# The block of w_q that lies on few partitions: 32 partitions and 4 steps instead of 16 and 8

## The chip, the cores and the metric

The kernel runs on one core of a Trainium2 chip. The metric is the device time of one execution in microseconds (us). A measured change of 2% in either direction counts as faster or slower.

## What is computed

One decode step for two sequences (B = 2) of width D = 448: a layer norm, grouped-query attention over a cache of 4096 keys (16 query heads of 256, 8 key/value heads), a bilinear feed-forward block whose SiLU gates the attention's result, and a residual.

```python
xn = layernorm(x)                                   # x: (2, 1, 448)
q = (xn @ wq).reshape(2, 1, 16, 256)                # wq: (448, 4096)
p = softmax(q . k_cache * 256 ** -0.5)              # k_cache, v_cache: (2, 8, 4096, 256)
s = (p . v_cache).reshape(2, 1, 4096) @ wo          # wo: (4096, 448)
g = silu(((xn @ w_gate) * (xn @ w_up)) @ w_down)    # F = 1792
out = x + s * g
```

All data is float32, some 158.5 MB of it, and almost all of that is the two caches.

## The kernel before

Each of the 16 pairs (key/value head, sequence) is a step of the main loop. Step i needs the tile of its values and the tile of the next step's keys. Both come in one load of 8 MB, `vk[i]`, of 128 partitions by 64 KB, into a `ring` of two buffers. The weights come through one buffer, `slot`, one after the other: w_q for the first half of the heads (`wq0`), w_gate and w_up (`wgu`), w_down (`wd`), w_q for the second half (`wq1`), and w_o (`wo`). All these loads are issued by SyncE (SP) at line 73 in one fixed order, which is the list `todo` (lines 83 to 91): wq0, first keys, vk0, wgu, vk1, vk2, wd, vk3, vk4, wq1, vk5, vk6, vk7, vk8, wo, vk9 to vk13, and then the last keys and values in pieces. A load is issued when the buffer that it goes to is free, that is when the matmuls that read that buffer's former content are done. A load that has to wait keeps those behind it on SP waiting too.

The instructions of every engine stand in the order in which the code records them (a manual schedule). In step i of the loop (line 312) TensorE runs the matmuls of `values(i)` (line 269), those of `scores(i + 1)` (line 238) and the small ones of the softmax. Then the next `ring` load may go, since both halves of its buffer have been read. After step 4 comes `query(1)`, the projection of the second half of the heads, which reads `wq1` out of `slot`.

`query` calls `rows` (line 163). D = 448 is cut into 3 blocks of 128 rows (k = 0, 1, 2) and one of 64, and the 2048 columns of one half into NT = 4 blocks of 512, one for each group of 32 columns of the PE array, so that four matmuls of 32 output columns can be in the array beside each other. For the second half one of these blocks, k = 2 and c = 0 (rows 256 to 383), isn't loaded with the others. It isn't in `wq1`, which has 13 blocks instead of 14, and lies in DRAM in an array of its own, `wqx`, folded onto SIDE = 16 partitions and EXTRA = 8 steps. It is loaded behind `wq1`'s columns in the same buffer (line 77) and multiplied in 8 matmuls of 16 rows each (line 174), all in column group 0, with `xeT`, the transposed rows of xn that belong to them. `xeT` is written once at the start, by 8 transposes of TensorE (line 136) and a copy of VectorE (line 137).

In DRAM, `wqx` has groups of rows with a row of padding behind each group, so that the load's source has the groups as its outer dimension: 4 groups of 4 rows of 16 KB each.

Of the kernel before, what the change touches and what calls it, by code (L numbers as in the profile page):

```python
# [26 lines left out]
LATE = 24  # L27
THIRD = [24, 25, 26, 28, 29, 30, 31, 27]
PART = 28 * FC
EXTRA = 8  # L30
SIDE = 16
EPS = 1e-5


# [5 lines left out]
def gated_decode_block(ctx: ExitStack, tc: tile.TileContext, x, first, vk, last0, last1, wq0, wq1, wqx, wo, wgu, wd, out):  # L40
    nc = tc.nc
# [7 lines left out]
    def bank(name="t", bufs=1):  # L49
        return psum.tile([128, 512], F32, name=name, bufs=bufs)  # L50
# [8 lines left out]
    loaded = {}  # L59
    todo = []  # L60

    def issue(n=1):
        for names, src, cuts in todo[:n]:
            weight = names[0].startswith("w")
            if weight:
                t = slot.tile([128, PART], F32, name="slot", align_bytes=512)
            else:
                t = ring.tile([128, 2 * ROW], F32, name="ring", align_bytes=512)
            width = ROW if not weight else PART // len(names)
            for i, name in enumerate(names):  # L70
                loaded[name] = t[:, i * width:(i + 1) * width]
            for lo, hi in zip(cuts, cuts[1:]):
                nc.sync.dma_start(t[:, lo:hi], src[:, lo:hi])  # L73
            if names == ["wq1"]:
                at = src.shape[1]
                loaded["wqx"] = t[:, at:at + EXTRA * 512]
                nc.sync.dma_start(loaded["wqx"][:SIDE], wqx[:, :4])
        del todo[:n]

    def plan(names, src, cuts=None):  # L80
# [9 lines left out]
    plan(f"k{LAST + 1} v{LAST}", last0, [0, ROW, 2 * ROW])  # L90
    plan(f"v{LAST + 1} wo2", last1, [0, 4096, 7168, *(ROW + i * D for i in (0, 3, 5, 7, 8))])
    issue(3)


# [36 lines left out]
    oT1 = const.tile([128, 3, 2, REP, W], F32)  # L131
    xeT = oT1[:SIDE].rearrange("p g d r m -> p (g d r) m")[:, :EXTRA]
    pt = bank()
    for j in range(EXTRA):
        at = 256 + j * SIDE
        nc.tensor.transpose(pt[:SIDE, B * j:B * (j + 1)], xn[:, at:at + SIDE], ident[:B, :B])
    nc.vector.tensor_copy(xeT.rearrange("p k (b j) -> p k b j", b=B),
                          pt[:SIDE, :EXTRA * B].rearrange("p (k b) -> p k b", b=B)[:, :, :, None].to_broadcast([SIDE, EXTRA, B, DUP]))

# [23 lines left out]
    def rows(ps, w, n, extra=None):  # L163
# [6 lines left out]
        for k in range(3):  # L170
            for c in range(NT):
                if extra is not None and (k, c) == (2, 0):
                    for j in range(EXTRA):
                        nc.tensor.matmul(ps[:W, :n], xeT[:, j, :], extra[:SIDE, j * n:(j + 1) * n], start=False, stop=False)  # L174
                    continue
# [132 lines left out]
    oT2 = const.tile([128, 1, 2, REP, W], F32)  # L308
    ss = scores(0)
    issue(2)  # L310
    p = over(softmax(*ss))
    for i in range(LAST):
        g, b = divmod(i, B)
        o = bank("o", 1)
        values(i, p[0], o)
        ss = scores(i + 1)

        issue(1 + (i + 1 in weights))
        nc.scalar.activation(ob[:, b * 4 + g if g < 4 else b * 3 + g - 4], o, AF.Copy, scale=p[1])  # L319
        if i == LAST - 1:  # L320
            cb = combine(ob, 6)
        p = softmax(*ss)
        if i < LAST - 1:
            p = over(p)
        if i == 7:
            cb = combine(ob, 8)
            for n in range(B):
                turn(oT0, cb[:, n * 256:(n + 1) * 256], 0, n, 4)
            ob = work.tile([128, 8, 512], F32, name="ob", bufs=1)
        if i in weights:  # L330
            if i == 0:
                ffn_in()
            if i == 2:
                ffn_out()
            if i == 4:
                query(1)
            if i == 8:
                project(oT0, 0, 0, EARLY)
# [78 lines left out]
```

## Time and profile before

| | us |
|---|---|
| median of 3 runs | 377.04 (376.45 to 396.36) |
| the profiled execution's own time | 377.45 |
| its span, first to last instruction | 375.7 |
| TensorE busy | 218.1 (58% of the span) |
| VectorE busy | 63.4 (17%) |
| ScalarE busy | 36.3 (10%) |

The span is what the views of the profile divide up; 1.75 us of the execution's own time lie outside it. A float32 matmul shows as two matmul instructions, so the 8 matmuls of line 174 are counted as 16. A load is named in the views by the buffer that it writes and the array that it reads: `ring<-vk`, `slot<-wq`, `slot<-wqx`.

### The profile page before, as it was taken

The page shows a single profiled execution, that of the slowest core. Times are in us where ns is not written, and L with a number is a line of the kernel's source. Part 1 is how long each engine was busy: PE and PEld are TensorE (multiplying, and loading weights), DVE is VectorE, ACT ScalarE, POOL GpSimd, SP SyncE. Part 2 cuts the span into 40 slices and gives each one's busy share as a digit, 9 for nine tenths or more (in the row PEclk, how much of TensorE's full clock was granted, in tenths as well). Part 3 has the DMA queues.
Part 4 walks back from the last instruction along what each step waited for, and adds up shares of the span by engine and source line. Part 5 has one row for each costly group of instructions (what it writes and reads, how often), then busy time and mean ns, then how long its engine had stood idle before and what let it go on. Part 6 is the DMA issues. An engine that isn't in the chain of part 4 may idle for free.

```text
span 375.7 us, 3266 instructions
## 1 busy us (share of the span) xinstructions
PE 218.1 (58%) x1470; PEld 64.2 (17%) x1470; DVE 63.4 (17%) x113; ACT 36.3 (10%) x56; POOL 1.2 (0%) x7
## 2 busy tenths in 40 slices
PE   1650649083861919699783766622827181919785
PEld 1110112021210202121121212200212021202232
DVE  4012030103030030300213030300121112030330
ACT  1001010001012020100111010100010101010120
POOL 1000000000000000000000000000000000000000
PEclk9986697667786776655967788965858685768899
DMA  8999999998999999999999999999999999999994
GB/s 342 440 461 391 441 447 447 447 441 386 430 434 447 440 405 484 426 405 440 434 433 426 420 433 405 455 447 433 440 420 434 447 412 426 448 412 429 419 417 163
DMA packets 4246, 158.74 MB, mean 423 GB/s; under 512 B 503, under 2 KB 633, under 8 KB 1145
## 3 DMA queue, kind: packets, MB, share of 16 engines
q1 hardware_dynamic: 4228, 158.54, 98.1%
q8 instruction: 11, 0.18, 0.2%
q14 instruction: 3, 0.02, 0.0%
q10 hardware_dynamic: 4, 0.00, 0.0%
HBM read 158.54 MB, written 0.01 MB: 422 GB/s over the span
## 4 chain that ended last, share of the span: by engine, by line
DMA 71%; PE 25%; SPq 1%; DVE 1%; issue 0%; ACT 0%; ACTq 0%
DMA ring<-vk 66%; PE o L269 12%; PE s L238 7%; DMA ring<-last 6%; PE t L174 4%; PE t L176 1%; SPq L73 1%; PE t L179 0%; DVE m L239 0%; ACT p L253 0%; PE acc L302 0%; DVE mx L246 0%; PE sm L261 0%; DVE h L366 0%; PE sm L244 0%
## 5 line engine op out<-in xcount | busy, mean ns | idle before, releaser
L269 PE MATMUL o<-ring,pT 128*32 128x512 f32 x480 | 83.0, 854 | 80.1 <-DMA ring<-vk 79.3
L238 PE MATMUL s<-ring,qT 128*32 128x512 f32 x512 | 61.0, 618 | 4.8 <-DMA ring<-first 3.3
L239 DVE TENSOR_REDUCE m<-s 128x1 f32<-128x1024 f32 x16 | 19.6, 1225 | 211.6 <-PE s L238 211.6
L269 PEld LDWEIGHTS o<-ring,pT 128*32 128x32 f32 x480 | 21.0, 150 | 133.5 <-issue 132.7
L319 ACT ACTIVATE ob<-o,su 128x512 f32<-128x512 f32 x14 | 9.6, 688 | 194.9 <-PE o L269 194.9
L253 ACT ACTIVATE p<-s,m 128x1024 f32<-128x1024 f32 x16 | 17.8, 1114 | 94.5 <-DVE m L250 94.5
L238 PEld LDWEIGHTS s<-ring,qT 128*32 128x32 f32 x512 | 17.8, 114 | 45.6 <-issue 44.0
L255 DVE STREAM_TRANSPOSE pT<-p 128x1024 f32<-128x1024 f32 x16 | 19.9, 1245 | 22.5 <-ACT p L253 22.5
L261 PE MATMUL sm<-su,add_head 128*128 128x1 f32 x32 | 7.8, 312 | 22.9 <-ACT p L253 22.9
L244 PE MATMUL sm<-ident,m 128*1 128x128 f32 x16 | 4.3, 270 | 18.9 <-DVE m L239 18.8
L174 PE MATMUL t<-slot,oT 16*32 16x512 f32 x16 | 13.9, 1056 | 0.0
L176 PE MATMUL t<-slot,xnT 128*32 128x512 f32 x46 | 10.9, 1059 | 4.0 <-DMA slot<-wq 4.0
L246 DVE TENSOR_REDUCE mx<-sm 1x128 f32<-1x512 f32 x16 | 10.9, 679 | 6.3 <-PE sm L244 6.3
L249 PE MATMUL sm<-one,mx 1*128 1x1 f32 x16 | 3.6, 223 | 12.3 <-DVE mx L246 12.3
L261 PEld LDWEIGHTS sm<-su,add_head 128*128 128x128 f32 x32 | 6.4, 249 | 25.1 <-ACT p L253 24.1
L176 PE MATMUL s<-slot,xnT 128*32 128x448 f32 x48 | 7.2, 747 | 2.7 <-DMA slot<-wgu 2.7
L244 PEld LDWEIGHTS sm<-ident,m 128*1 128x1 f32 x16 | 1.3, 79 | 33.0 <-DVE m L239 32.3
L188 DVE STREAM_TRANSPOSE qT<-t 128x256 f32<-128x256 f32 x4 | 1.6, 428 | 31.0 <-PE t L179 31.0
L296 PE MATMUL wide<-slot,oT 128*32 128x448 f32 x48 | 6.6, 701 | 0.0
L278 PE MATMUL cb<-ob,add_blocks 128*32 128x64 f32 (+2 forms) x64 | 5.9, 496 | 0.8 <-ACT ob L358 0.8
L220 PE MATMUL t<-slot,hT 128*32 128x448 f32 x28 | 4.9, 810 | 0.0
L249 PEld LDWEIGHTS sm<-one,mx 1*128 1x128 f32 x16 | 2.2, 139 | 15.4 <-DVE mx L246 15.4
(68 smaller groups left out, 54.5 us busy)
## 6 DMA issues: line engine op xcount, KB each, us to landing
ring<-last SPq DMA_DIRECT2D x2, 4096.0 KB, 24.2
slot<-wgu SPq DMA_DIRECT2D x1, 6272.0 KB, 38.5
slot<-wo SPq DMA_DIRECT2D x1, 5376.0 KB
ring<-first SPq DMA_DIRECT2D x1, 4096.0 KB, 20.3
slot<-wq SPq DMA_DIRECT2D x1, 3584.0 KB, 11.0
slot<-wq SPq DMA_DIRECT2D x1, 3328.0 KB, 35.6
slot<-wd SPq DMA_DIRECT2D x1, 3136.0 KB, 36.9
ring<-last SPq DMA_DIRECT2D x1, 2048.0 KB
```

The costliest lines, as they stand in the source:

```text
L174: nc.tensor.matmul(ps[:W, :n], xeT[:, j, :], extra[:SIDE, j * n:(j + 1) * n], start=False, stop=False)
L176: nc.tensor.matmul(ps[W * c:W * (c + 1), :n], xnT[:, k, :], block(NT * k + c), start=k == 0, stop=False)
L238: nc.tensor.matmul(s[W * c:W * (c + 1), h, :], q[:, d], k[:, h, d, c, :], start=d == 0, stop=d == 1)
L239: nc.vector.tensor_reduce(m[:, 0:1], s, axis=AX.XY, op=OP.max)
L246: nc.vector.tensor_reduce(mx, sm[:1, None, :128].rearrange("p o (c j) -> p o j c", c=NT).to_broadcast([1, NT, W, NT]), axis=AX.X, op=OP.max)
L253: nc.scalar.activation(p, s, AF.Exp, bias=m[:, 1:2], scale=1.0 / 16, accum_out=su[:, 0:1])
L255: nc.vector.transpose(pT.rearrange("p h n -> p (h n)"), p.rearrange("p h n -> p (h n)"))
L261: nc.tensor.matmul(sm[:, 130:131], add_head.rearrange("p a r j -> p (a r j)"), su[:, 0:1], start=True, stop=True)
L269: nc.tensor.matmul(o[W * t:W * (t + 1), :], pT[:, h, at:at + 2 * W:2], loaded[f"v{i}"][:, e * 512:(e + 1) * 512], start=e < NT, stop=e >= ...
L278: nc.tensor.matmul(cb[W * c:W * (c + 1), :n * 64], add_blocks[:, e].rearrange("p r j -> p (r j)"), src[:, :n, e, :, c, :], start=e == 0, s ...
L296: nc.tensor.matmul(wide[W * t:W * (t + 1), :D], heads(oT, i, first), loaded["wo"][:, i * D:(i + 1) * D], start=i < NT, stop=i >= LATE - NT)
L319: nc.scalar.activation(ob[:, b * 4 + g if g < 4 else b * 3 + g - 4], o, AF.Copy, scale=p[1])
```

## The change

SIDE goes from 16 to 32 and EXTRA from 8 to 4, and the number of groups, which was SIDE // 4 = 4, gets a name of its own, GROUPS = 4. The block keeps its 128 rows by 512 columns, 256 KB. It is now 4 groups of 8 rows of 8 KB each, with one row of padding behind each group, on partitions 0 to 31. Four matmuls of 32 rows take the place of 8 of 16, and 4 transposes that of 8.

```diff
-EXTRA = 8
-SIDE = 16
+EXTRA = 4
+SIDE = 32
+GROUPS = 4
@@ issue
-                nc.sync.dma_start(loaded["wqx"][:SIDE], wqx[:, :4])
+                nc.sync.dma_start(loaded["wqx"][:SIDE], wqx[:, :SIDE // GROUPS])
@@ kernel
-    wqx = np.zeros((SIDE // 4, 5, EXTRA * 512), np.float32)
-    wqx[:, :4] = wq1[:, 8 * 512:9 * 512].reshape(EXTRA, SIDE // 4, 4, 512).transpose(1, 2, 0, 3).reshape(SIDE // 4, 4, EXTRA * 512)
+    n = SIDE // GROUPS
+    wqx = np.zeros((GROUPS, n + 1, EXTRA * 512), np.float32)
+    wqx[:, :n] = wq1[:, 8 * 512:9 * 512].reshape(EXTRA, GROUPS, n, 512).transpose(1, 2, 0, 3).reshape(GROUPS, n, EXTRA * 512)
```

The order of the instructions on every engine and the semaphores that each load waits for stay as they were.

## The prediction

> **What bounds the kernel now.** I read the page's slices and its table of DMA queues first, to see whether the transfers ever rest.
>
> ```profile
> DMA  8999999998999999999999999999999999999994
> q1 hardware_dynamic: 4228, 158.54, 98.1%
> q8 instruction: 11, 0.18, 0.2%
> DMA 71%; PE 25%; SPq 1%; DVE 1%; issue 0%; ACT 0%; ACTq 0%
> ```
>
> They don't: the 16 DMA engines are busy in every slice up to the last. Queue q1, which holds the loads, takes 98.1% of 16 engines' span. That is 0.981 x 375.7 x 16 = 5897 us of engine time for 158.54 MB, so one engine moves 26.9 KB per us and all sixteen 430 KB. The end comes when the engine with the most to do has done it. The chain of waits says 25% TensorE, but that is not time in which the transfers stood still. To see where TensorE's work reaches them I read the chain in order of time around the changed block.
>
> ```profile
> 156.17 3.57 PE t L176 x16
> 159.74 13.79 PE t L174 x16
> 173.53 1.86 PE t L176 x6
> 175.38 1.86 PE t L179 x8
> 177.25 3.87 PE o L269 x32
> 181.12 3.49 PE s L238 x32
> 184.61 0.02 issue
> 184.62 24.59 DMA ring<-vk
> ```
>
> Columns: start, length, what. Line 174, the block on few partitions, takes 13.79 us of TensorE, and the values and scores behind it (L269, L238) release a ring buffer only at 184.61. The load that goes there is vk7 in the order of the list: it is issued at 184.62 and has landed 24.59 us later. A vk load is 8.39 MB, 19.5 us at 430 KB per us, so 5.1 us are left for what stood before it and for the start. How long a start takes on idle engines is seen at the kernel's first load.
>
> ```profile
> 0.74 0.39 SPq L73
> slot<-wq SPq DMA_DIRECT2D x1, 3584.0 KB, 11.0
> ```
>
> The first load of w_q, 3.67 MB or 8.5 us of flow, landed 11.0 us after its issue, so 2.5 us go to the start and to the spread of the engines. Of vk7's 5.1 us that leaves 2.6 us of older work on the engine that finished last. The transfers were nearly out of work when it was issued. The windows of 5 us around it show it in the last column (GB/s):
>
> ```profile
> 164.00:169.00 5.00, 5.00 (x7) 0.97 (x6) 0.00 (x0) 0.00 (x0) 0.00 (x0) 0.50 0.97 419
> 179.00:184.00 5.00, 5.00 (x52) 1.32 (x44) 0.00 (x0) 0.69 (x1) 0.00 (x0) 1.00 0.99 423
> 184.00:189.00 5.00, 1.32 (x12) 0.50 (x4) 2.37 (x4) 1.21 (x2) 0.00 (x0) 0.91 0.97 367
> 189.00:194.00 5.00, 4.26 (x22) 1.37 (x26) 0.99 (x2) 0.00 (x0) 0.00 (x0) 0.50 0.97 419
> ```
>
> From 184 to 189 the flow is 367 against 419 to 423 on both sides: 54 x 5 = 270 KB fewer than at 421, or 0.6 us of all engines. It is a dip in a flow that is elsewhere steady, and the only place where TensorE's work in this kernel costs transfer time.
>
> **The change, part by part.** First TensorE.
>
> ```profile
> L174 PE MATMUL t<-slot,oT x16: 1056/1056/1057, 159.7 to 172.5; 16*32 16x512 f32 x16
> L176 PE MATMUL t<-slot,xnT x22: 1057/1057/1062, 156.1 to 174.3; 128*32 128x512 f32 x22
> L179 PE MATMUL t<-slot,xnT x8: 1057/1058/1059, 175.3 to 176.2; 64*32 64x512 f32 x8
> ```
>
> An instruction on 16, 64 or 128 rows takes the same (1056, 1058, 1057 ns), so one on 32 rows does too. The 16 instructions of line 174 follow each other in one column group, 13.79 / 16 = 0.86 us apart; 8 fewer take 6.9 us away. The values would then start at 177.25 - 6.9 = 170.3 if their load has landed.
>
> ```profile
> 113.95 0.33 SPq L73 DMA_DIRECT2D slot<-wq  x1
> 114.33 0.82 SPq L77 DMA_DIRECT2D slot<-wqx  x1
> 131.61 68.28 SPq L73 DMA_DIRECT2D ring<-vk  x4
> ring<-vk SPq DMA_DIRECT2D x2, 38.6
> slot<-wqx SPq DMA_DIRECT2D x1, 256.0 KB
> ```
>
> vk5 and vk6, the two of the fourth row, take 38.6 us in the median. vk5, issued at 131.61, lands near 170.2, just in time. The buffer comes free near 177.7, vk7 is issued 6.9 us earlier, and stands behind work that lasts some 9 us instead of 2.6. So the dip goes. Its worth lies between nothing (if it is only the grain of 64 KB rows in windows of 5 us) and the 2.5 us of a whole start. I take the measured 0.6 us as a mean over the engines, and 0.3 us for those that carried wqx, since their queue was the fuller one. Behind that the next thing late is the transfers themselves.
>
> The rest of what TensorE, VectorE and SP lose or gain is covered. The 4 transposes and the smaller copy lie at the start, where TensorE then waits 4.01 us for the first weights:
>
> ```profile
> 6.33 0.34 PE L136 MATMUL t<-ident,pT 2*16 2x2 f32 x8 [0.38 <-DVE xnT L127]
> 11.92 1.08 PE L176 MATMUL t<-slot,xnT 128*32 128x512 f32 x4 [4.01 <-DMA slot<-wq]
> ```
>
> They are worth at most 0.34 us, inside that wait; if the cover were gone they would be a gain of 0.2 us. The issue of wqx took SP 0.82 us from 114.33; with 32 rows instead of 16 it could take twice that, or less than now. SP's next issue comes at 131.61, so up to 16 us of cover stand behind it.
>
> Now the load itself, where the profile of before has no row for the new form. Its 256 KB stay 256 KB. Over four engines that is 65.5 KB each, 65.5 / 26.9 = 2.44 us; over sixteen it would be 0.61 us, over two 4.9 and over one 9.7 us. The 2.6 us that vk7's slowest engine still had in front of it are nearest to four, and exclude two and one. So today four engines run 2.44 us behind the others from the wqx load on. With 4 groups as the outer dimension again, I take four engines again, and as many bytes on each. What differs is where they write: 8 neighbouring partitions each instead of 4, and partitions 16 to 31 are new. While they do, the other twelve engines go on with vk5, each into its own partitions. If what limits the flow is the engine, an engine may write anywhere at 26.9 KB per us, and the price is 0. If what limits it is the receiving side, where two engines meet on the same partitions they have half of it each. Then an engine whose whole 65.5 KB are shared needs 4.88 us, 2.44 us more, and the engine that it meets loses 1.2 us. Those are the ends, 0 and +2.44 us on some of the four; every window shows a full flow with every engine in its own partitions, and so no row is near either end. I take the upper end, for two of the four engines: the rows of groups 2 and 3 go to partitions that no wqx row went to before, where other engines are writing vk5.
>
> The Trainium skill speaks against the change here: its page "SBUF — State Buffer", section "Door 1: The DMA port swizzle", says that four neighbouring partitions (with the four 32 above) lie behind one of 16 ports of about 27.2 GB/s each, and measures 27.6 GB/s for a load to partitions 0 to 3 and 104 GB/s for one to 0 to 15. By it the old load meets only the ports of its own engines, and the new one those of four others: the sum is then the upper end, and without it the lower one. No run here shows it yet.
>
> What of 2.44 us reaches the end is read from the last microseconds of transfer.
>
> ```profile
> 350.27 21.14 DMA ring<-last
> 371.40 0.04 issue
> 368.00:369.00 1.00, 0.73 (x6) 0.00 (x0) 0.00 (x0) 0.23 (x1) 0.00 (x0) 1.00 0.91 355
> 369.00:370.00 1.00, 0.49 (x28) 0.49 (x32) 0.00 (x0) 0.46 (x1) 0.00 (x0) 1.00 0.74 294
> 370.00:371.00 1.00, 1.00 (x40) 0.65 (x28) 0.25 (x1) 0.00 (x0) 0.00 (x0) 1.00 0.34 133
> 371.00:371.50 0.50, 0.13 (x8) 0.05 (x8) 0.00 (x0) 0.00 (x0) 0.00 (x0) 1.00 0.10 36
> ```
>
> From 368 on 355 + 294 + 133 + 18 = 800 KB flow, 1.9 us at 430. The mean engine thus ends near 369.9 and the last at 371.4: 1.5 us of slack for an engine in the middle, none for the last. The four carriers are among the late ones, since they had 2.44 us more to do; against that the 11 instruction fetches of q8 (0.2% of 5897 us, some 1 us each) fall on single engines too. An engine in the middle would push the end by 2.44 - 1.5 = 0.9 us, the last one by 2.44. I take the middle, 1.7 us, less the 0.3 us that the carriers gain at 184: +1.4 us. The work behind the last landing, from 371.4 to 375.7, is unchanged.
>
> Sum for the profiled execution: 377.45 + 1.4 = 378.85 us. That execution is 0.41 us above the median of the runs, 377.04, so I forecast 378.4 for the median.
>
> **Rivals.** First, faster: the receiving side isn't the limit and four engines write at full speed. For it speaks that no row of this trace shows two engines held up at one place; against it that none could, since every load so far gives each engine partitions of its own. Then only the dip at 184 goes: 377.04 - 0.6 = 376.4, with 376.0 to 376.8 for a gain of 0.3 to 1.0.
>
> Second, slower by more: the load falls on fewer engines than four. It decides as soon as one engine holds all of it: 9.7 us instead of 2.44, +7.3 us, less 0.9 of mean slack and gain is 6.4, so 383.4. For it speaks only that rows and groups are no longer equal in number (8 and 4); against it that the outer dimension is 4 as before. The Trainium skill, "DMA: Bandwidth & Descriptors", section "Why a DMA increments its semaphore by 16 and not by 1", gives a load the largest number of engines up to 16 that divides both outer dimensions, here 4 and 32, so 4 as with 4 and 16; the landing of vk7 agrees for the old one.
>
> Third, nothing shows: no sharing, and the dip at 184 stays because it comes with each late issue or is only grain: 377.0.
>
> **How the numbers follow.** The forecast with sharing has 0.64, the faster rival 0.28, no effect 0.05, fewer engines 0.03. The forecast's own range is 0.9 - 0.3 to 2.44 on the median, 377.6 to 379.5. To hold 8 in 10 the range takes in the faster rival down to 376.0 and ends at 379.5; what is left out is the fewer engines and the outer ends of the others. A measurement of this kernel can tell about 2%, 7.5 us, from no change. None of the main cases reaches that on either side: within 2% has 0.97. Faster by that would need the transfers to gain 7 us where the dip holds at most 2.5: 0.01. Slower by that needs the load on one engine and no slack at all: 0.02.
>
> **What would show it.** Line 174's matmuls, 8 instructions in some 6.9 us instead of 13.79. vk7 issued near 178 if vk5 lands at 170.2, near 180 if it lands 2.4 us later as sharing would have it. The window of 184 to 189 back at some 420 GB/s. The tail of the flow behind 370: with sharing longer and thinner by one to two us, the last landing near 372.8; without it the last landing near 370.8. The forecast is wrong if the tail ends earlier than now, and the whole reasoning is if the flow shows a stop elsewhere.

## The result

The changed kernel takes 378.83 us (median of 6 runs, 378.72 to 379.10) against 376.98 us for the kernel before, measured beside it: a ratio of 1.0048 with a 95% interval of 1.0033 to 1.0064. That is 1.8 us slower, clear of the noise and well inside 2%. The forecast was 378.4. One of the six runs of the kernel before took 396.36 us, a slow run that the ratio leaves out.

The profiled execution took 379.07 us, with a span of 377.3. Its flow of transfers first, in the windows around the load of wqx and around 184 us (columns: window, length, busy time and instructions of PE, PEld, DVE, ACT and POOL, clock, DMA share, GB/s). The kernel after:

```profile
147.00:153.00 6.00, 4.27 (x41) 1.11 (x33) 1.57 (x2) 0.69 (x1) 0.00 (x0) 1.00 1.12 348
184.00:189.00 5.00, 0.60 (x3) 0.43 (x3) 1.71 (x4) 1.20 (x2) 0.00 (x0) 0.79 0.97 419
```

The kernel before, in the first of these windows:

```profile
147.00:153.00 6.00, 4.66 (x44) 1.16 (x35) 1.22 (x1) 0.69 (x1) 0.00 (x0) 0.99 1.15 496
```

While wqx is loaded the flow is 348 GB/s instead of 496, 148 x 6 = 890 KB less in these 6 us, or 2.1 us of all engines at 430. (The view counts a transfer's bytes in one place, so that a window of a few us can be off by some 15%.) At 184, where the kernel before had 367, it is now 419: that dip is gone. The transfer records of the trace say the same more finely. They have the start, the length and the bytes of every row of a load, but don't name the engine. With the bytes spread evenly over each row's time, the flow in the first window is 316 GB/s instead of 432, or 1.6 us of all engines. From 147 to 154 the rows took 30.1 us of engine time more than rows of their size take undisturbed (2.42 us for a vk row of 64 KB), 1.88 us per engine, against 0.003 before; from 184 to 190 it was 0.003, against 0.63 before.

TensorE's side, from the chain of waits and the timeline of the kernel after:

```profile
131.18 41.77 DMA ring<-vk
172.95 0.14 issue
173.09 5.40 PE o L270 x32
178.49 3.47 PE s L239 x32
181.96 0.02 issue
181.98 29.57 DMA ring<-vk
```

```profile
155.47 2.97 PE L177 MATMUL t<-slot,xnT 128*32 128x512 f32 x16
158.36 7.03 PE L175 MATMUL t<-slot,oT 32*32 32x512 f32 x8
165.32 1.93 PE L177 MATMUL t<-slot,xnT 128*32 128x512 f32 x6
167.18 1.93 PE L180 MATMUL t<-slot,xnT 64*32 64x512 f32 x8
173.09 5.40 PE L270 MATMUL o<-ring,pT 128*32 128x512 f32 x32 [3.97 <-DMA ring<-vk]
```

The block on few partitions takes 7.0 us instead of 13.8, and the projection is done at 169.1. But vk5, issued at 131.18, lands only at 172.95, so that TensorE waits 4.0 us for it. The buffer comes free at 181.96, 2.65 us earlier than before, and the load that is issued then lands 29.57 us later instead of 24.59: there is work in front of it again.

The end, from the same chain and from windows of 1 us:

```profile
351.44 21.59 DMA ring<-last
373.04 0.04 issue
```

```profile
368.00:369.00 1.00, 0.99 (x10) 0.38 (x12) 0.22 (x1) 0.00 (x0) 0.00 (x0) 1.00 1.02 419
369.00:370.00 1.00, 1.00 (x12) 0.15 (x6) 0.00 (x0) 0.00 (x0) 0.00 (x0) 1.00 0.92 366
370.00:371.00 1.00, 0.30 (x2) 0.00 (x0) 0.00 (x0) 0.65 (x1) 0.00 (x0) 1.00 0.71 271
371.00:372.00 1.00, 0.91 (x40) 0.76 (x40) 0.25 (x1) 0.04 (x1) 0.00 (x0) 1.00 0.39 152
372.00:373.00 1.00, 0.67 (x21) 0.38 (x16) 0.00 (x0) 0.00 (x0) 0.00 (x0) 1.00 0.16 63
```

The last landing is at 373.04 instead of 371.40, 1.64 us later, and the tail behind 370 holds 271 + 152 + 63 = 486 KB where it held some 150. The span grew by 1.6 us.

### The profile page after: what moved, and what is told of

It reads as the page before. It is cut to its first block, busy times and chain, and to the rows that moved or that the text cites. A ratio compares the mean times of both kernels' runs of the same rounds, so it can differ in the third digit from the quotient of the medians.

```text
span 377.3 us, 3242 instructions
## 1 busy us (share of the span) xinstructions
PE 212.3 (56%) x1458; PEld 63.1 (17%) x1458; DVE 63.2 (17%) x113; ACT 36.2 (10%) x56; POOL 1.2 (0%) x7
## 4 chain that ended last, share of the span: by engine, by line
DMA 74%; PE 21%; another core or an unknown queue 3%; SPq 1%; issue 0%; DVE 0%
DMA ring<-vk 55%; PE o L270 11%; DMA slot<-wgu 10%; PE s L239 6%; DMA ring<-last 6%; DMA slot<-wq 3%; PE s L177 2%; PE t L177 1%; SPq L74 1%; PE s L180 0%; PE t L180 0%; PE acc L303 0%; DVE h L367 0%; DVE h L368 0%
## 5 line engine op out<-in xcount | busy, mean ns | idle before, releaser
L270 PE MATMUL o<-ring,pT 128*32 128x512 f32 x480 | 86.5, 886 | 88.1 <-DMA ring<-vk 87.2
L239 PE MATMUL s<-ring,qT 128*32 128x512 f32 x512 | 59.7, 607 | 5.4 <-DMA ring<-first 3.8
L177 PE MATMUL t<-slot,xnT 128*32 128x512 f32 x46 | 9.8, 953 | 4.2 <-DMA slot<-wq 4.2
L175 PE MATMUL t<-slot,oT 32*32 32x512 f32 x8 | 7.0, 1056 | 0.0
```

The costliest lines, as they stand in the source:

```text
L177: nc.tensor.matmul(ps[W * c:W * (c + 1), :n], xnT[:, k, :], block(NT * k + c), start=k == 0, stop=False)
L239: nc.tensor.matmul(s[W * c:W * (c + 1), h, :], q[:, d], k[:, h, d, c, :], start=d == 0, stop=d == 1)
L270: nc.tensor.matmul(o[W * t:W * (t + 1), :], pT[:, h, at:at + 2 * W:2], loaded[f"v{i}"][:, e * 512:(e + 1) * 512], start=e < NT, stop=e >= ...
```

## The experiments

Four theories were open: that engines hold each other up where they write the same partitions (A); that rows of 8 KB, or 32 of them, are dear in themselves (B); that the shorter TensorE stage disturbs the transfers (C); and, within A, whether only the engines that meet lose, as I had priced it, or all (A2).

**The same 32 partitions from 8 groups.** The changed kernel with

```diff
-GROUPS = 4
+GROUPS = 8
```

> The changed kernel with 8 groups of 4 rows instead of 4 groups of 8: the same 32 partitions, 4 matmuls and rows of 8 KB, but, if the groups set the number of engines, eight engines with 4 neighbouring partitions each. Theory A (two engines meet at the partitions that one of them regularly writes): as in the old load every engine writes only partitions of its own, so the flow from 147 to 153 us is near 490 GB/s as before and not 348 as in the changed kernel, and the dip at 184 stays away: 376.0 to 376.6 us. Theory B (rows of 8 KB, or 32 of them, are dear in themselves): the loss stays, about 378.8 us. Theory C (the shorter TensorE stage itself disturbs the transfers): about 378.8 us.

Measured: 376.77 us, 0.9996 of before (0.998 to 1.0012).

```profile
147.00:153.00 6.00, 3.96 (x37) 1.03 (x29) 1.89 (x2) 0.69 (x1) 0.00 (x0) 1.00 1.07 464
184.00:189.00 5.00, 0.46 (x4) 0.23 (x8) 0.00 (x0) 0.00 (x0) 0.00 (x0) 0.50 1.00 433
```

All 32 rows of 8 KB take 309 ns in the transfer records, none is held up, and no vk row is. They follow each other in eight chains, so eight engines now spend 4 x 0.31 = 1.2 us each on the load. So neither the 32 partitions, nor the rows of 8 KB, nor the 4 matmuls cost more than the 0.5 us that the interval leaves: B and C fall, and the loss is gone with the one number that says which engine writes which rows. That number also sets how many engines carry the load, eight instead of four; the loads to four places further down keep four. The gain of 0.1 to 0.7 us over the kernel before that I expected isn't seen, though the interval would still hold one of 0.8.

**Rows of 8 KB on the old 16 partitions.** The kernel before with its load cut into two:

```diff
-                nc.sync.dma_start(loaded["wqx"][:SIDE], wqx[:, :4])
+                for lo in (0, EXTRA * 256):
+                    nc.sync.dma_start(loaded["wqx"][:SIDE, lo:lo + EXTRA * 256], wqx[:, :4, lo:lo + EXTRA * 256])
```

> The kernel before with its wqx load cut into two, columns 0 to 2047 of each row and then 2048 to 4095: 32 rows of 8 KB on partitions 0 to 15, and TensorE's 8 matmuls as before. Theory A (engines meeting at partitions): flow from 147 to 153 us near 490 GB/s, 377.0 us within 0.5. Theory B (the size or number of the rows): flow near 350 there, 378.5 to 379 us.

Measured: 376.82 us, 1.0001 (0.9992 to 1.0010).

```profile
147.00:153.00 6.00, 4.30 (x41) 1.14 (x33) 1.54 (x2) 0.69 (x1) 0.00 (x0) 1.00 1.16 501
184.00:189.00 5.00, 1.07 (x4) 0.71 (x4) 2.79 (x5) 1.20 (x2) 0.00 (x0) 0.82 0.98 419
```

```profile
183.42 25.48 DMA ring<-vk
```

501 GB/s: B falls a second time. The second window and the line of its chain of waits show something else. TensorE works as long here as in the kernel before, and yet there is next to no dip at 184 (0.04 us per engine in the records). The buffer came free at 183.42 here and at 184.61 there. The kernel before stands just on the edge: 1.2 us decide whether the loss at 184 comes. Engines without work are the smaller part of it. In the records of the kernel before, from 184 to 190, 10.0 us of engine time went into rows that lasted longer (up to 4.05 us instead of 2.42), and from 186 to 188 some 1.7 us into engines that had no row. Why the rows lasted longer there isn't shown.

**The load and the matmuls apart.** First the new load with TensorE's time as before, by issuing the 4 matmuls of line 175 twice:

```diff
+                    for j in range(EXTRA):
+                        nc.tensor.matmul(ps[:W, :n], xeT[:, j, :], extra[:SIDE, j * n:(j + 1) * n], start=False, stop=False)
```

> The changed kernel's load, with its 4 matmuls of line 175 issued twice, so that TensorE works as long there as before; that block of w_q is counted twice in the queries. Theory A: flow from 147 to 153 us near 350 GB/s as in the changed kernel; all engines then have 1.9 us more of old work, so the late issue of vk7 costs less than the 0.6 us of before: 378.8 to 379.4 us. Theory C (the shorter TensorE stage disturbs the transfers): 377.0 us and no loss at 147.

Measured: 378.84 us, 1.0056 (1.0040 to 1.0071), with the loss at the same place:

```profile
147.00:153.00 6.00, 4.89 (x44) 1.29 (x36) 1.04 (x1) 0.69 (x1) 0.00 (x0) 0.93 1.13 348
```

Then the old load with half of the matmuls:

```diff
-                    for j in range(EXTRA):
+                    for j in range(EXTRA // 2):
                         nc.tensor.matmul(ps[:W, :n], xeT[:, j, :], ...
```

> The kernel before with its own load, and only 4 of the 8 matmuls of line 174; the other half of that block is left out of the queries. Theory A: the flow from 147 to 153 us stays near 490 GB/s, the dip from 184 to 189 us goes, 376.4 us (376.0 to 376.8). If the dip was only grain: 377.0 us. Theory C: 378.8 us.

Measured: 376.59 us, 0.9994 (0.9984 to 1.0003).

```profile
147.00:153.00 6.00, 4.66 (x45) 1.24 (x37) 1.23 (x1) 0.69 (x1) 0.00 (x0) 1.00 1.16 501
184.00:189.00 5.00, 0.00 (x0) 0.00 (x0) 0.87 (x2) 0.00 (x0) 0.00 (x0) 0.55 1.00 433
```

The load alone is the whole change, and 6.9 us of TensorE are worth at most 0.6 us and perhaps nothing: the interval takes in 1.

**Only the partitions differ.** The kernel before with one more load behind wqx that nothing reads, the same 112 KB from the same place, to partitions P to P + 15 with P = 0, 16, 32, 64:

```diff
+                nc.sync.dma_start(t[P:P + SIDE, at + EXTRA * 512:at + EXTRA * 512 + 1792], wqx[:, :4, :1792])
```

> The kernel before with one more load behind wqx that nothing reads: 4 groups of 4 rows of 7 KB (112 KB in all) from the same array, to partitions 0 to 15 in columns further on. Theory A (an engine is slowed when it writes partitions that another engine regularly writes; partitions 0 to 15 belong to the four engines themselves): 28.7 KB more on four engines, 1.07 us each, no slowed rows; flow from 147 to 153 us near 490 GB/s; 377.0 to 378.1 us. Any theory by which only the bytes, rows and engines of a load count gives this one and the next three the same time.

> As the last, but the unread load goes to partitions 16 to 31. Theory A: these belong to four other engines; the changed kernel sent 128 KB there and lost 1.9 us per engine in the mean, so 112 KB lose some 1.6: flow from 147 to 153 us near 370 GB/s, 378.2 to 379 us. By bytes alone: as with partitions 0 to 15.

> As the last, but to partitions 32 to 47. Theory A with the rule that partitions 32 to 47 lie with 0 to 15: as with partitions 0 to 15, flow near 490 GB/s, 377.0 to 378.1 us. If it is a matter of low partitions, or of a load that isn't at partition 0: as with 16 to 31.

> As the last, but to partitions 64 to 79, which belong to four engines of the other half. Theory A: as with 16 to 31, flow near 370 GB/s and 378.2 to 379 us. By bytes alone: as with partitions 0 to 15.

Measured, against 376.58 us for the kernel before, with the GB/s of the window from 147 to 153 and the engine time lost in held-up rows from 147 to 154, summed over the transfer records:

| extra load to partitions | us | ratio (95%) | GB/s | lost, us per engine |
|---|---|---|---|---|
| 0 to 15 | 377.95 | 1.0029 (1.0013 to 1.0045) | 483 | 0.00 |
| 16 to 31 | 379.55 | 1.0067 (1.0050 to 1.0085) | 404 | 1.36 |
| 32 to 47 | 377.81 | 1.0024 (1.0005 to 1.0043) | 487 | 0.00 |
| 64 to 79 | 379.58 | 1.0064 (1.0040 to 1.0088) | 404 | 1.16 |

The rows of the windows for 0, 16, 32 and 64, each from its own kernel:

```profile
147.00:153.00 6.00, 3.89 (x38) 1.01 (x30) 1.90 (x2) 0.69 (x1) 0.00 (x0) 1.00 1.12 483
```

```profile
147.00:153.00 6.00, 4.34 (x41) 1.15 (x33) 1.50 (x2) 0.69 (x1) 0.00 (x0) 1.00 1.16 404
```

```profile
147.00:153.00 6.00, 4.47 (x41) 1.15 (x33) 1.38 (x2) 0.69 (x1) 0.00 (x0) 1.00 1.13 487
```

```profile
147.00:153.00 6.00, 4.61 (x45) 1.15 (x33) 1.23 (x2) 0.69 (x1) 0.00 (x0) 1.00 1.12 404
```

The flow is less disturbed than the 370 that I expected, and the times are up to 0.6 us above the range, but the order is A's: same bytes, rows, number of engines and source, and only the place decides. The two dear places cost 1.6 us more than partitions 0 to 15. Partitions 32 to 47 behave like 0 to 15, as the Trainium skill has it ("SBUF — State Buffer", section "Door 1: The DMA port swizzle": the partitions 32 above share a port). A place of its own costs the four engines 4 rows of 272 ns, 1.09 us each; a foreign one costs everyone. That the four engines of these loads are those that write partitions 0 to 15 and 32 to 47 in a vk load is read off these four results; no view names the engines.

**How many meetings, and who pays.** Three more unread loads behind wqx in the kernel before:

```diff
# one engine
+                nc.sync.dma_start(t[16:33, ...], wqx.rearrange("g r n -> (g r) n")[:17, :1792])
# two engines
+                nc.sync.dma_start(t[16:32, ...], wqx.rearrange("(a b) r n -> a (b r) n", a=2)[:, :8, :1792])
# four engines, three of which meet only each other's free places
+                nc.sync.dma_start(t[4:20, ...], wqx[:, :4, :1792])
```

> The kernel before with an unread load of 17 rows of 7 KB (119 KB) behind wqx, to partitions 16 to 32. 17 has no divisor but itself, so if the engines are chosen by the row counts, one engine carries all of it, 17 x 0.27 = 4.5 us alone and up to 9 us where it has to share, and meets one other engine at a time. Theory A as I priced it (only the engines that meet lose): vk rows of 64 KB stay at 2.42 us except those of the engine that is met; flow at worst 434 - 27 = 407 GB/s; that one engine ends 4.5 to 9 us later, so 379.5 to 385 us. Theory A2 (a meeting holds up all engines that load at that time): nearly all vk rows of these microseconds are longer than 2.5 us. If the load isn't on one engine: as with the load to partitions 16 to 31 before, 379.5 us.

> As the last, with 2 groups of 8 rows of 7 KB (112 KB) to partitions 16 to 31: two engines, 57 KB each, 2.1 us alone and up to 4.3 shared, two meetings at a time. Theory A (only those that meet lose): 4 engines of 16 have longer rows, flow at worst 434 - 54 = 380 GB/s. Theory A2 (all are held up): nearly all rows are longer, and the sum of the lost engine time is near that of the four-engine load to the same partitions (22 us) or above. Time: 379 to 381 us by both.

> As the four-engine unread loads (4 groups of 4 rows of 7 KB, 112 KB), to partitions 4 to 19: engines 0 to 2 write partitions of engines 1 to 3, which are themselves moved on by four and so leave them free, and only the fourth meets an engine that goes on with vk. Theory A: nearly no loss, vk rows stay at 2.42 us but for one engine's, 377.8 to 378.5 us. Theory A2: one meeting holds up all, rows up to 2.7 us for 1 to 2 us, 378 to 378.8 us. If every write outside an engine's own partitions is dear, whoever else writes there: as with partitions 16 to 31, 379.5 us and flow near 290 GB/s in its worst microseconds.

Measured, against 376.60 us: 385.06 (1.0224, 1.0194 to 1.0254), 380.37 (1.0100, 1.0070 to 1.0129) and 379.44 (1.0075, 1.0046 to 1.0104). The windows from 149 to 155, one from each kernel in this order:

```profile
149.00:155.00 6.00, 3.07 (x26) 0.80 (x18) 2.06 (x3) 0.53 (x1) 0.00 (x0) 0.90 1.10 432
```

```profile
149.00:155.00 6.00, 2.34 (x23) 0.57 (x15) 2.09 (x4) 1.21 (x2) 0.00 (x0) 1.00 1.05 339
```

```profile
149.00:155.00 6.00, 2.34 (x24) 0.84 (x20) 2.46 (x4) 1.20 (x2) 0.00 (x0) 1.00 1.10 451
```

and, for comparison, the kernel before, and the four engines that went to partitions 16 to 31:

```profile
149.00:155.00 6.00, 2.92 (x26) 0.74 (x18) 2.06 (x3) 0.68 (x1) 0.00 (x0) 0.91 1.10 475
```

```profile
149.00:155.00 6.00, 2.56 (x22) 0.61 (x14) 2.06 (x3) 1.04 (x2) 0.00 (x0) 1.00 1.00 341
```

One engine that meets one other: in the records its 17 rows follow each other and take 272 ns at first, then 520 to 580 with a shorter one now and then, 8.05 us from the first start to the last end instead of 4.6. It ends so late that it sets the end alone: from 376 to 378 the flow is 26 GB/s, about what one engine moves, and the whole takes 8.5 us more. At 156 us, when 15 vk rows were in flight, all 15 were longer than usual, thirteen by 0.27 to 0.39 us and two by 1.2 to 1.3. So even one meeting is felt by all, but little: the flow, the records' bytes spread evenly over each row's time, was 364 to 405 GB/s from 151 to 158 beside 434 undisturbed. Two engines with two meetings: 271 to 301 for four microseconds, 14 of 14 vk rows in flight at 152 longer, most by 1.3 to 1.7 us. Four meetings are no worse than two (277 to 303 in the worst three microseconds with partitions 16 to 31, 294 to 341 with 64 to 79). So A2 holds: the engines that share get half, and from two meetings on the flow of all sixteen falls by about a third at its worst.

The load shifted by four gives a flow of 451 with 0.39 us lost per engine from 147 to 154, where the same load to partitions 16 to 31 lost 1.36. In its worst four microseconds the flow by the records is 383 to 415, as with the one meeting above. It isn't writing outside an engine's own partitions that is dear, but writing where another engine is writing. The time of the shifted load, 379.44, is nevertheless above both ranges: the records show one engine finishing its last vk row 1.7 us after the next one (340.3 and 338.6 us), which fits the fourth engine with its own share, its slowed rows and wqx behind each other. The last windows of this kernel fit too, with the rate of about one engine:

```profile
372.00:373.00 1.00, 1.00 (x44) 0.76 (x32) 0.25 (x1) 0.00 (x0) 0.00 (x0) 1.00 0.08 30
373.00:374.00 1.00, 0.59 (x25) 0.35 (x16) 0.00 (x0) 0.00 (x0) 0.00 (x0) 1.00 0.05 18
```

Which engine it is the trace doesn't name, and the load to partitions 64 to 79 also ends with one engine 1.7 us behind the next (341.1 and 339.4 us), so the cause of the late engine isn't shown.

## Why the prediction was right, and where its sum was not

**TensorE.** The 4 matmuls took 7.0 us, and the forecast of 6.9 less held. vk5 landed at 172.95 and vk7 was issued at 181.98: with sharing I had said 2.4 us later than 170.2 and near 180. The order of causes was right and the landing of vk5 forecast 0.4 us too early. The values then took 5.40 us instead of 3.87, which I had not counted; the granted clock while they ran was 0.67, and 0.92 in the kernel before.

**The dip at 184.** It went, as forecast, in the profiled execution: 0.63 us per engine before, 0.003 after. But its worth was taken from one execution and then counted on the median. The median of before is 0.4 to 0.9 us below that execution, the load in halves shows next to no dip with the same TensorE work, and the halved matmuls alone gain 0.2 us with an interval that takes in nothing. And the prediction saw in it transfers that were nearly out of work, where most of the loss was rows that lasted longer. The first rival's 376.4 rested on this 0.6 us. The kernel with eight groups has what that rival asks for, full speed (on eight engines) and the short TensorE stage, and its ratio of 0.9996 (0.998 to 1.0012) puts the rival at 376.9, without excluding 376.4.

**The load.** The mechanism that I chose as the likelier one is shown: the place alone makes the difference (16 to 31 against 32 to 47), and removing the meetings removes the whole loss (eight groups). The term that was mis-sized is who pays. The prediction had the upper end of 2.44 us on two of the four engines, and 1.2 us on each engine that they meet. The records give 4.9 us more for the 32 wqx rows together, which is those 2 x 2.44; but the vk rows beside them lost 24.6 us where four engines with 1.2 would have made 4.8. All engines were held up, not only those that were met: at 151 us all 14 vk rows in flight were longer, by 0.9 to 1.8 us. The prediction put the loss of the engines that aren't met at nothing.

**From the load to the end.** I took +1.7 us for a late engine, less 0.3. Measured was 1.64 us at the last landing, but by another way. The mean engine lost 1.88 us at the load, not the 0.6 of my account (two times 2.44 and four times 1.2, over 16), and got back the 0.63 at 184. The tails show it: behind 368 us the kernel before has some 800 KB to move and the changed one 1276 (419 + 366 + 271 + 152 + 63 and 5 behind 373), so that the mean engine ends 1.1 us later. Only the other 0.5 us come from the last engine's being further behind the mean. My account had nothing for the mean engine, 0.6 lost and 0.6 regained, and all of its 1.4 in the late engine. That the sum came near was luck in this step. The median moved by 1.8 us, where the forecast had 1.4.

**The rivals.** That no sharing occurs fell with the partitions' experiment. That the load falls on fewer engines is not what happened: the records of the changed kernel show four rows of 8 KB going at a time. The price that I gave for one engine, 383.4, looks low, though no run put this load on one engine: the 17 rows brought only 119 KB more to one engine and came to 385.06, since they went at half the rate for most of the time, which wasn't in that sum.

## What to carry to other kernels

When transfers bound a kernel, look at a small load not only for its bytes but for which DMA engine writes which partitions. In these runs a load on few partitions was free of charge beyond its bytes when each engine wrote the partitions that it writes in the large loads (4 neighbouring ones here); a second engine on the same partitions cost all engines for as long as it lasted. And before a dip in one profiled execution is counted as a gain, see whether the median of the runs has it at all.

## What I hadn't expected of the hardware

An engine that shares a place gets half, 520 to 580 ns instead of 272 for a row of 7 KB, as one would think. But the other engines, which write elsewhere, slow down too: with two or four such pairs the flow of all sixteen falls from 434 to between 271 and 341 GB/s in the worst three microseconds, with one pair to between 364 and 415. Two pairs lower the flow as much as four. What these engines share that fills up was not tried and stays open.
